# Attention decode over two caches: wo one place further on in the load queue, one exp a tile with a masked copy, both q in SBUF, score sums two chunks behind

## The chip, the cores and the metric

The kernel runs on one core of one Trainium2 chip. The time is the device time of one execution in microseconds (us). Medians of several executions are given, beside executions of the kernel before on the same chip in the same rounds. The engines are PE (TensorE matmul), PEld (its weight loads), DVE (VectorE), ACT (ScalarE), POOL (GpSimd) and SP, whose queue (SPq) issues the loads.

## The reference

Two independent attention layers, A and B, each with its own input, caches and weights. For each of 8 batch rows there is one query position, 32 heads of 128, and a cache of 4096 keys and values per head, all in bf16.

```python
def _A_ref(x, k_cache, v_cache, wq, wo):          # B is the same
    q = (x @ wq).reshape(B, 1, H, Dh).transpose(0, 2, 1, 3)
    scores = einsum("bhqd,bhkd->bhqk", q, k_cache) * (Dh ** -0.5)
    p = softmax(scores, axis=-1)
    o = einsum("bhqk,bhkd->bhqd", p, v_cache)
    return o.transpose(0, 2, 1, 3).reshape(B, 1, H * Dh) @ wo
return concatenate([a, b], axis=-1)
```

Nearly all of the 1.1 GB that the kernel reads are the two caches, and each byte of them is used once.

## The kernel before

The work is cut into 64 tiles, n = 0 to 63 (0 to 31 are cache A). A tile is 8 heads of one batch row: a K tile and a V tile, each of 128 partitions x 64 KB, 8.39 MB. SBUF holds three slots of that size. Two take K tiles in turn (and now and then a weight), the third takes V tiles (the very last V tile goes into a K slot). All loads go through one queue, in the order of a plan that is laid down at the start. A load is issued when the last reader of its slot is done, and a load that has to wait holds up all loads behind it in the plan.

The plan before. The output weight `wo` of a cache takes a K slot, once its last full block of tiles is done. The last K tile and the last V tile are loaded in pieces (`cuts`), and between the pieces of the last V comes `wo8`, the rows of wo for the last 8 heads:

```python
put("wq", 0, 1)
put("k", 0)
put("wq", 1, 2)
for n in range(NQ - 1):
    if n + 2 < NQ:
        put("k", n + 1)
    else:
        put("k", n + 1, cuts=((0, NR // 2), (NR // 2, NR)))
    for c in range(NC):
        if n == done_at(c, NC, HB, B) + 1:        # n = 32 for A, 56 for B
            put("wo", c)
            late[n] = c
    put("v", n, 2)
put("v", NQ - 1, cuts=((0, NR // 2),))
put("wo8", 0, 2)                                  # into the V slot
plan.append(("v", NQ - 1, ((NR // 2, 3 * NR // 4), (3 * NR // 4, 7 * NR // 8), (7 * NR // 8, NR))))
```

The load of a tile. `opT[(kind, n, r)]` is the load that a reader of chunk r (of 8) has to await:

```python
for r0, r1 in cuts or ((0, NR),):
    cols = slice(r0 * CT * Dh, r1 * CT * Dh)
    op = dma(to[:, cols], from_[:, cols], (kind + "l", r0) if cuts else key, [dep])
    for r in range(r0, r1):
        opT[(kind, n, r)] = op
...
elif kind == "wo":
    rows = wo_rows(n)                             # 128 for A, 96 for B
    opT[(kind, n)] = dma(to[0:rows, 0:H * D], caches[n][4][0:rows * H, :].rearrange("(p r) n -> p (r n)", r=H), key, [dep])
```

A K tile in 8 chunks: DVE multiplies by q (`ring<-ring,qbc`) and folds 128 to 64, PE sums 64 to 16 into PSUM (`red`), DVE sums the rest (`s_sb<-red`). Two `red` banks are used in turn, and DVE sums a chunk right after it has multiplied the next one. When the tile is done, DVE finds a shift for the softmax, and ACT writes the weights of the tile in eight passes, one for each head, masked by scale and bias:

```python
for j in range(HQ):                               # HQ = 8
    e.activation(PM[:, :, j], s_sb[:, n % 2, :], ACTF.Exp, bias=bias[:, n % 2, j:j + 1],
                 scale=own_sc[:, j:j + 1], accum_out=rsum[:, blk % 2, b, j:j + 1])
```

PV of tile n (64 matmuls of PM with V) runs on PE at chunk 5 of tile n + 1, and the V slot is then free. PV of the last tile runs in four parts, each of which awaits its piece of V:

```python
for g0, g1 in ((0, 8), (8, 12), (12, 14), (14, 16)):
    make_pv(n, g0 * RG // 16, g1 * RG // 16)      # awaits opT[("v", n, g1 * NR // RG - 1)]
```

## Time and profile before

| | before |
|---|---|
| time, median (lowest to highest) of 3 | 2605.85 us (2604.26 to 2607.56) |
| span of the profiled execution | 2604.0 us |
| read from HBM | 1107.3 MB |
| DVE / PE / ACT busy | 81% / 48% / 26% |

Four lines of the page: busy time of the engines; the share of the load engines in tenths and the GB/s that they moved, both in 40 slices of 65 us; and their packets and bytes in all.

```profile
PE 1256.4 (48%) x8130; PEld 387.1 (15%) x8130; DVE 2103.5 (81%) x1807; ACT 675.6 (26%) x1169; POOL 5.7 (0%) x23
...
DMA  9999999999999999999999999999999999999997
GB/s 420 430 433 433 435 431 432 432 430 434 433 434 432 434 435 433 432 432 432 433 406 434 434 432 433 432 433 432 429 433 435 433 432 434 421 320 432 433 426 324
DMA packets 20840, 1108.61 MB, mean 426 GB/s; under 512 B 2272, under 2 KB 2336, under 8 KB 3376
```

The DMA row is at 9 in all slices but the last, and the rate stays at 429 to 435 GB/s but for the first slice, slice 21 (406, A's wo), slices 35 and 36 (421 and 320, B's wo) and the last two. The Trainium skill, "DMA: Bandwidth & Descriptors", "Where 436 GB/s comes from", puts the ceiling of the 16 ports at 435.2 GB/s; the trace agrees, with 433 for hundreds of us. The same section says that for loads from HBM a lower limit, about 358 GB/s, binds; in this trace it did not. So the kernel is bound by its loads.

Three of the groups (line, engine, operation, out<-in, shapes, count | busy us, mean ns of one | idle us before, and on whom):

```profile
L315 DVE TENSOR_TENSOR ring<-ring,qbc 128x4096 bf16<-128x4096 bf16 x512 | 1169.7, 2284 | 334.5 <-DMA ring<-in_B_k_cache_dram 168.8 <-DMA ring<-in_A_k_cache_dram 165.7
...
L356 ACT ACTIVATE PM<-s_sb,bias,own_sc 128x256 bf16<-128x256 f32 x512 | 609.4, 1608 | 935.2 <-DVE bias L349 935.2
L337 DVE TENSOR_REDUCE s_sb<-red 128x32 f32<-128x512 f32 x512 | 350.2, 684 | 126.1 <-PE red L329 126.1
```

DVE waits 334.5 us for K tiles and 126.1 us for PE. ACT's eight exps of a tile are 1.6 us each, and they overlap.

Stretches of the span (from:to, length, busy us of the five engines with instruction counts, granted PE clock, DMA share, GB/s):

```profile
600.00:1000.00 400.00, 194.15 (x1249) 59.35 (x1250) 337.87 (x290) 108.72 (x191) 0.00 (x0) 0.60 1.00 433
1315.00:1320.00 5.00, 3.58 (x57) 1.59 (x50) 3.94 (x4) 0.60 (x1) 0.00 (x0) 1.00 0.84 357
1320.00:1325.00 5.00, 2.10 (x8) 0.51 (x6) 4.97 (x5) 0.00 (x0) 0.00 (x0) 0.93 0.54 236
...
1360.00:1365.00 5.00, 1.04 (x4) 0.31 (x4) 1.12 (x2) 0.00 (x0) 0.00 (x0) 1.00 0.97 419
2275.00:2280.00 5.00, 2.10 (x8) 0.53 (x5) 4.92 (x5) 0.00 (x0) 0.00 (x0) 0.66 0.36 157
...
2290.00:2295.00 5.00, 2.70 (x6) 0.72 (x7) 5.00 (x5) 4.68 (x10) 0.00 (x0) 0.50 0.98 210
...
2330.00:2335.00 5.00, 1.57 (x16) 0.70 (x20) 0.00 (x0) 0.00 (x0) 0.00 (x0) 0.50 0.97 419
2572.00:2576.00 4.00, 1.86 (x12) 0.68 (x10) 3.23 (x3) 0.41 (x1) 0.00 (x0) 1.00 0.79 286
2576.00:2580.00 4.00, 1.41 (x4) 0.43 (x4) 2.53 (x3) 0.00 (x0) 0.00 (x0) 0.62 1.10 412
```

The load engines idle for a few us at 1315 to 1325 and 2275 to 2280, just before A's and B's wo are issued, and a little at 2572. While B's wo is loaded (2280 to 2310, one line of it is shown) they are as busy as ever, but at 210 GB/s.

The moments at which a K tile has landed can be read from DVE, because DVE waits for almost every one: the first multiply of a tile starts when it lands. These are tiles 56, 57, 58 and 59, with B's wo between 57 and 58 (columns: start, us, what, idle before and on whom):

```profile
2242.31 2.29 DVE L315 TENSOR_TENSOR ring<-ring,qbc 128x4096 bf16<-128x4096 bf16 x1 [4.31 <-DMA ring<-in_B_k_cache_dram]
...
2280.99 2.29 DVE L315 TENSOR_TENSOR ring<-ring,qbc 128x4096 bf16<-128x4096 bf16 x1 [1.03 <-DMA ring<-in_B_k_cache_dram]
...
2352.83 2.29 DVE L315 TENSOR_TENSOR ring<-ring,qbc 128x4096 bf16<-128x4096 bf16 x1 [29.76 <-DMA ring<-in_B_k_cache_dram]
...
2391.54 2.29 DVE L315 TENSOR_TENSOR ring<-ring,qbc 128x4096 bf16<-128x4096 bf16 x1 [3.84 <-DMA ring<-in_B_k_cache_dram]
```

An ordinary interval is 38.7 us, the time of one K and one V. Across B's wo it is 71.8 us.

And the end of the span, in order of time (first the two PV of tiles 62 and 63 and the issue of wo8 between them; then the first and the last exp of tile 63, from ACT's own timeline):

```profile
2566.23 5.54 PE L368 MATMUL pv<-ring,PM 128*32 128x512 bf16 x64 [1.45 <-DMA ring<-in_B_v_cache_dram]
...
2571.81 0.38 SPq L162 DMA_DIRECT2D ring<-in_B_wo_dram  x1
...
2592.60 6.00 PE L368 MATMUL pv<-ring,PM 128*32 128x512 bf16 x64
```

```profile
2582.48 1.52 ACT L356 ACTIVATE PM<-s_sb,bias,own_sc 128x256 bf16<-128x256 f32 x1 [10.07 <-DVE bias L349]
...
2590.32 1.60 ACT L356 ACTIVATE PM<-s_sb,bias,own_sc 128x256 bf16<-128x256 f32 x1
```

The last exp ends near 2592, after the loads have ended (about 2590); only then comes the last PV, 6.0 us for all 64 matmuls.

### The profile page before, as it was taken

The page shows a single profiled execution, that of the slowest core. Times are in us where ns is not written, and L with a number is a line of the kernel's source. Part 1 is how long each engine was busy: PE and PEld are TensorE (multiplying, and loading weights), DVE is VectorE, ACT ScalarE, POOL GpSimd, SP SyncE. Part 2 cuts the span into 40 slices and gives each one's busy share as a digit, 9 for nine tenths or more (in the row PEclk, how much of TensorE's full clock was granted, in tenths as well). Part 3 has the DMA queues.
Part 4 walks back from the last instruction along what each step waited for, and adds up shares of the span by engine and source line. Part 5 has one row for each costly group of instructions (what it writes and reads, how often), then busy time and mean ns, then how long its engine had stood idle before and what let it go on. Part 6 is the DMA issues. An engine that isn't in the chain of part 4 may idle for free.

```text
span 2604.0 us, 19575 instructions
## 1 busy us (share of the span) xinstructions
PE 1256.4 (48%) x8130; PEld 387.1 (15%) x8130; DVE 2103.5 (81%) x1807; ACT 675.6 (26%) x1169; POOL 5.7 (0%) x23
## 2 busy tenths in 40 slices
PE   3554454454454454455454544544545544543454
PEld 1111111111111111111111111111111111111111
DVE  3788888888888888889886888888888888857885
ACT  1223223223223223213312232232232232213133
POOL 0000000000000000000000000000000000000000
PEclk8665665665665665665566556656656656655666
DMA  9999999999999999999999999999999999999997
GB/s 420 430 433 433 435 431 432 432 430 434 433 434 432 434 435 433 432 432 432 433 406 434 434 432 433 432 433 432 429 433 435 433 432 434 421 320 432 433 426 324
DMA packets 20840, 1108.61 MB, mean 426 GB/s; under 512 B 2272, under 2 KB 2336, under 8 KB 3376
## 3 DMA queue, kind: packets, MB, share of 16 engines
q1 hardware_dynamic: 20656, 1107.32, 99.1%
q8 instruction: 63, 1.03, 0.2%
q14 instruction: 25, 0.20, 0.0%
q10 hardware_dynamic: 96, 0.05, 0.0%
HBM read 1107.33 MB, written 0.03 MB: 425 GB/s over the span
## 4 chain that ended last, share of the span: by engine, by line
DMA 53%; DVE 32%; PE 13%; ACT 2%; issue 1%; DVEq 0%
DMA ring<-in_A_k_cache_dram 26%; DMA ring<-in_B_k_cache_dram 24%; DVE ring L315 16%; DVE ring L320 10%; PE pv L368 6%; PE red L329 6%; DVE s_sb L337 5%; ACT PM L356 1%; DMA ring<-in_B_wo_dram 1%; DMA ring<-in_B_v_cache_dram 1%; DMA ring<-in_A_wq_dram 1%; PE q L279 1%; DVE rmax L343 1%; DVE rtmp L345 0%; DVE bias L349 0%
## 5 line engine op out<-in xcount | busy, mean ns | idle before, releaser
L329 PE MATMUL red<-ring,ident 128*128 128x512 bf16 x2048 | 851.3, 562 | 1265.3 <-DVE ring L320 1265.3
L315 DVE TENSOR_TENSOR ring<-ring,qbc 128x4096 bf16<-128x4096 bf16 x512 | 1169.7, 2284 | 334.5 <-DMA ring<-in_B_k_cache_dram 168.8
L356 ACT ACTIVATE PM<-s_sb,bias,own_sc 128x256 bf16<-128x256 f32 x512 | 609.4, 1608 | 935.2 <-DVE bias L349 935.2
L320 DVE TENSOR_TENSOR ring<-ring 128x2048 bf16<-128x2048 bf16 x512 | 621.9, 1215 | 0.0
L329 PEld LDWEIGHTS red<-ring,ident 128*128 128x128 bf16 x2048 | 204.3, 121 | 1807.6 <-DVE ring L320 1541.8
L337 DVE TENSOR_REDUCE s_sb<-red 128x32 f32<-128x512 f32 x512 | 350.2, 684 | 126.1 <-PE red L329 126.1
L368 PE MATMUL pv<-ring,PM 128*32 128x512 bf16 x4096 | 318.0, 479 | 16.6 <-DMA ring<-in_B_v_cache_dram 16.6
L356 ACT ACTIVATION_READ_ACCUMULATOR PM<-s_sb,bias,own_sc 128x1 f32 x512 | 256.0, 500 | 0.0
L376 ACT ACTIVATE accS<-pv 128x512 bf16<-128x512 f32 x64 | 38.2, 597 | 819.7 <-PE pv L368 819.7
L368 PEld LDWEIGHTS pv<-ring,PM 128*32 128x32 bf16 x4096 | 121.5, 118 | 233.7 <-issue 178.8
L305 ACT ACTIVATE qbc<-misc 128x128 bf16<-128x128 f32 x64 | 17.8, 278 | 136.3 <-PE misc L300 136.3
L389 PE MATMUL o<-accS,E 128*32 128x32 bf16 x896 | 31.7, 177 | 0.0
L279 PE MATMUL q<-ring,xT 128*8 128x512 bf16 x128 | 26.1, 423 | 11.2 <-DMA ring<-in_A_wq_dram 11.2
L389 PEld LDWEIGHTS o<-accS,E 128*32 128x32 bf16 x896 | 25.9, 94 | 24.2 <-ACT accS L376 23.3
L343 DVE TENSOR_REDUCE rmax<-s_sb 128x1 f32<-128x256 f32 x64 | 26.9, 420 | 2.2
L300 PE MATMUL misc<-q_sb,selb 8*32 8x128 bf16 x512 | 26.2, 295 | 0.8 <-ACT q_sb L288 0.8
L345 DVE TENSOR_SCALAR rtmp<-half,rmax 128x32 f32<-128x32 f32 x64 | 15.4, 241 | 2.3
L288 ACT ACTIVATE q_sb<-q 8x512 bf16<-8x512 f32 x16 | 9.3, 603 | 30.7 <-PE q L279 30.6
L300 PEld LDWEIGHTS misc<-q_sb,selb 8*32 8x32 bf16 x512 | 9.2, 103 | 53.9 <-issue 53.9
L349 DVE SCALAR_TENSOR_TENSOR bias<-own_sc,ngm,own_b 128x8 f32<-128x8 f32 x64 | 14.5, 226 | 2.3
L407 PE MATMUL o<-rsum,own_m 128*32 128x8 f32 x112 | 7.1, 202 | 18.2 <-ACT PM L356 18.2
L348 DVE TRANSPOSE_TENSOR_REDUCE ngm<-rtmp 128x1 f32<-128x32 f32 x64 | 13.5, 211 | 2.2
(37 smaller groups left out, 55.7 us busy)
## 6 DMA issues: line engine op xcount, KB each, us to landing
ring<-in_B_k_cache_dram SPq DMA_DIRECT2D x2, 4096.0 KB, 35.6
ring<-in_B_v_cache_dram SPq DMA_DIRECT2D x1, 4096.0 KB, 32.0
ring<-in_B_wo_dram SPq DMA_DIRECT2D x1, 2048.0 KB, 10.2
ring<-in_B_v_cache_dram SPq DMA_DIRECT2D x1, 2048.0 KB, 14.7
ring<-in_B_v_cache_dram SPq DMA_DIRECT2D x2, 1024.0 KB, 17.0
ring<-in_A_k_cache_dram SPq DMA_DIRECT2D x32, 41.3
ring<-in_A_v_cache_dram SPq DMA_DIRECT2D x32, 30.3
ring<-in_B_k_cache_dram SPq DMA_DIRECT2D x31, 41.0
```

Source lines behind the costliest of these rows:

```text
L279: i = e.matmul(q_ps[f][rows, :], xT[:, (c * DC + k) * B:(c * DC + k + 1) * B], w[:, col:col + 512], start=(k == 0), stop=(k == DC - 1), ti ...
L300: x = e.matmul(misc[32 * g:32 * (g + 1), 0:Dh], selb[rows, b, i, :], q_sb[rows, j * Dh:(j + 1) * Dh], start=(i == 0), stop=(i == 1), tile_ ...
L305: "act", lambda e: e.activation(qbc[:, n % 2, :], misc[:, 0:Dh], ACTF.Copy),
L315: opMul[s] = add("dve", lambda e: e.tensor_tensor(v, v, qbc[:, n % 2, :].unsqueeze(1).to_broadcast([128, CT, Dh]), ALU.mult), [opT[("k", n ...
L320: return add("dve", lambda e: e.tensor_tensor(v[:, :, 0:64], v[:, :, 0:64], v[:, :, 64:128], ALU.add), [opMul[s]])
L329: i = e.matmul(dst, ident[:], v[:, :, j, :], start=(j == 0), stop=(j == 3))
L337: opRed[s] = add("dve", lambda e: e.tensor_reduce(s_sb[:, n % 2, r * CT:(r + 1) * CT], red_ps[s % 2][:, :].rearrange("p (t w) -> p t w", w ...
L343: opRmax[n] = add("dve", lambda e: e.tensor_reduce(rmax[:], s_sb[:, n % 2, :], AX.X, ALU.max), [opRed[NR * n + NR - 1]])
L356: return e.activation(PM[:, :, j], s_sb[:, n % 2, :], ACTF.Exp, bias=bias[:, n % 2, j:j + 1], scale=own_sc[:, j:j + 1], accum_out=rsum[:, ...
L368: i = e.matmul(pv_ps[32 * q:32 * (q + 1), :], PM[:, t:t + 4, :].rearrange("p t j -> p (t j)"), v[:, t * Dh:(t + 4) * Dh], start=(g == 0), ...
L376: opAcc[n] = [add("act", lambda e: e.activation(accS[:], pv_ps[:], ACTF.Copy), [opPV[n], _at(opExt, n - 1)])]
L389: x = e.matmul(o_ps[MB * hb:MB * (hb + 1), H * b:H * (b + 1)], E[:, i, PH - 1 - u:PH - 1 - u + MB], accS[:, i * 128 + H * u:i * 128 + H * ...
```

## The change

In words: wo one place further on, behind the V tile; one exp a tile into `pe`, and a masked copy of it on DVE; q of both caches computed early and kept in SBUF; score sums two chunks behind, over four PSUM banks; PV in two halves. The intent is to take the wait of wo off the head of the queue, to shorten the softmax and to take DVE's waits for PE away. The diff, cut to what can touch the time:

```diff
@@ the plan @@
+            put("v", n, 2)
             for c in range(NC):
                 if n == done_at(c, NC, HB, B) + 1:
                     put("wo", c)
-                    late[n] = c
-            put("v", n, 2)
+                    late[n + 2] = c
@@ the loads @@
                     for r0, r1 in cuts or ((0, NR),):
                         ...
-                        for r in range(r0, r1):
+                        for r in range(H):
                             opT[(kind, n, r)] = op
@@ sums @@
-        red_ps = [ps(f"red{i}") for i in range(2)]
+        red_ps = [ps(f"red{i}") for i in range(4)]
...                                   # red of chunk s - 2 behind the multiply of chunk s (was s - 1)
@@ softmax @@
-            for j in range(HQ):
-                def emit(e, j=j):
-                    return e.activation(PM[:, :, j], s_sb[:, n % 2, :], ACTF.Exp, bias=bias[:, n % 2, j:j + 1],
-                                        scale=own_sc[:, j:j + 1], accum_out=rsum[:, blk % 2, b, j:j + 1])
+            opExp[n] = add("act", lambda e: e.activation(pe[:], s_sb[:, n % 2, :], ACTF.Exp, bias=ngm[:, n % 2:n % 2 + 1], scale=scale,
+                                                         accum_out=rsum[:, blk % 2, b:b + 1]), ...)
+            opPM[n] = add("dve", lambda e: e.tensor_tensor(PM[:], pe[:].unsqueeze(2).to_broadcast([128, T, HQ]),
+                                                           own_h[:].unsqueeze(1).to_broadcast([128, T, HQ]), ALU.mult), ...)
@@ row sums of the last block: eight matmuls instead of one @@
@@ PV @@
-        pv_at = {((n + 2, 0) if n in late else (n + 1, 5)): n for n in range(NQ - 1)}
+        pv_at = {(n + 1, 5): n for n in range(NQ - 1)}
-                if k == 0:
-                    make_pv(v, 0, RG)
-                    make_acc(v)
+                if k < 2:                         # half at chunk 5, half at chunk 6
+                    make_pv(v, k * RG // 2, (k + 1) * RG // 2)
@@ the product with wo @@
-            if r >= 5 and n - 1 in late:
-                i = r - 5
-                make_proj(late[n - 1], i * H // 3, (i + 1) * H // 3)
+            if r == 0 and n in late:
+                make_proj(late[n])
... # q of both caches: make_q interleaves the four head blocks, both caches at the start
```

## The prediction

> **What bounds the kernel now.** The stream from HBM. The page's DMA row shows 1108.6 MB; windows of 400 us in the middle move 432 to 433 GB/s at a DMA share of 1.00, so the bytes alone take about 2560 of the 2604 us span. DVE is busy 81%, PE 48%, ACT 26%. The timeline shows a tile pair (one K, one V) every 38.7 us. DVE works on a K tile for about 35 us, then waits for the next: 334.5 us in all (groups), some 4.6 us for an ordinary tile. The queue always has work: a K load is issued 41 us and a V load 30 us before it lands, with 22 and 11 us of other loads ahead of it. So a faster DVE, PE or ACT cannot show there.
>
> The other 44 us (narrow windows) are mostly:
> - B's wo load of 96 rows: 6.3 MB at 210 GB/s, DMA share near 1.0, 30 us in place of 14.5: 15.5 us lost. The change keeps it.
> - The queue running dry before each wo (share 0.54 at 1320 to 1325, 0.36 at 2275 to 2280): wo waits for the K tile in work, and V waits behind it. By the landings of K, about 2 us lost in A, 3 in B.
> - The tail: the last V lands near 2590, the span ends 14 us later. The last softmax ran eight exps in a row (9.5 us), so all of the last PV (6.0 us) came after the loads.
>
> **What the change does.**
> 1. wo behind V(n): V's 19 us cover the wait. Both dry spells go: -5 us.
> 2. Eight exps (1.14 us from start to start) become one, about 1.6 us: off the critical path but in the last tile.
> 3. The masked copy is a DVE tensor_tensor of 128x2048 whose first input repeats one element 8 times. The Trainium skill, "Vector Engine (DVE) Microarchitecture Reference", 5.1, measured such a stepless input at 1x. Nothing in this trace shows it; its 2x ops take 2284 ns for 4096 elements, so 2048 at 1x should take about 2.28 us: +146 us of DVE, less 14.5 us for the bias op.
> 4. Sums lagging two chunks over four PSUM banks: most of DVE's 126 us of waits for PE go. With 3, DVE per tile stays near 35 us of 38.7; busy rises to about 2235 us (86%).
> 5. PV in two halves: V is issued about 3.5 us later, against 11 us of cover.
> 6. q of both caches early: matmuls of four column groups interleave, 64 in about 6 us instead of 14.4. Hidden: K lands at 43 us.
> 7. Tail: exp 1.6 + copy 2.3 replace 9.5; the last lsum grows to eight fp32 matmuls (estimate 4 us, partly under the copy). PV ends 5 to 6 us earlier: -5.5 us.
>
> **Predicted: 2596 us**, range 2588 to 2604. Chances: faster by over 2% 1%, within 2% 97%, slower 2%.
>
> **What would show it right or wrong.** DMA share about 1.0 around both wo issues; wo of B still 30 us; middle windows still 433 GB/s; masked copy 2.28 us; DVE wait for K 4 to 5 us a tile; DVE waits for PE under 40 us; last V landing to the end about 8 us instead of 14.
>
> **What would make it wrong.** The later V issue meeting DMA engines that have run dry [...]: 1 us a tile gives 2650. A copy over 3.5 us would make DVE the limit.

## The result

| | before | after |
|---|---|---|
| time, median (lowest to highest) of 4 each | 2605.45 us (2604.26 to 2607.56) | 2612.85 us (2612.49 to 2613.43) |
| ratio | | 1.0028 (95% interval 1.001 to 1.0045) |
| span of the profiled execution | 2604.0 us | 2611.2 us |
| DVE busy | 2103.5 us | 2221.5 us |
| ACT busy | 675.6 us | 105.2 us |

A ratio is the mean time of one kernel's runs over the mean of the other's from the same rounds, so it is not quite the ratio of the medians. The change makes the kernel slower by 7.4 us, 0.28%, which is within 2% but outside the predicted 2588 to 2604.

The page after:

```profile
PE 1221.1 (47%) x8046; PEld 371.0 (14%) x8046; DVE 2221.5 (85%) x1805; ACT 105.2 (4%) x273; POOL 5.7 (0%) x23
...
GB/s 418 434 434 434 433 433 433 432 432 433 433 432 431 433 432 433 429 428 433 432 403 435 434 434 435 431 432 432 432 433 433 432 432 432 432 304 432 426 430 292
```

The rate is the same in the middle. It is lower than before in slice 36 (304 for 320), where B's wo is loaded, and in the last slice (292 for 324).

The groups that answer to those of before:

```profile
L311 DVE TENSOR_TENSOR ring<-ring,qbc 128x4096 bf16<-128x4096 bf16 x512 | 1169.3, 2284 | 351.8 <-DMA ring<-in_B_k_cache_dram 187.2 <-DMA ring<-in_A_k_cache_dram 164.6
...
L333 DVE TENSOR_REDUCE s_sb<-red 128x32 f32<-128x512 f32 x512 | 348.6, 681 | 1.4 <-PE red L325 1.4
...
L353 DVE TENSOR_TENSOR PM<-pe,own_h 128x2048 bf16<-128x2048 bf16 x64 | 146.2, 2284 | 0.7 <-ACT pe L347 0.7
...
L347 ACT ACTIVATE pe<-s_sb,ngm 128x256 bf16<-128x256 f32 x64 | 32.5, 509 | 1032.7 <-DVE ngm L344 1032.7
...
L347 ACT ACTIVATION_READ_ACCUMULATOR pe<-s_sb,ngm 128x1 f32 x64 | 11.9, 187 | 0.0
```

DVE's waits for PE have gone from 126.1 to 1.4 us. The masked copy takes 2284 ns, and the exp 0.51 us with 0.19 us for reading the accumulator. DVE still waits 351.8 us for K. The same stretches after (but for 2290 to 2295, with 2580 to 2584 added):

```profile
600.00:1000.00 400.00, 190.25 (x1221) 56.68 (x1222) 356.59 (x290) 15.04 (x41) 0.00 (x0) 0.60 1.00 434
1315.00:1320.00 5.00, 4.21 (x56) 1.72 (x54) 5.00 (x4) 0.60 (x1) 0.00 (x0) 1.00 1.06 459
1320.00:1325.00 5.00, 1.04 (x4) 0.31 (x4) 2.27 (x3) 0.00 (x0) 0.00 (x0) 0.89 0.97 419
...
1360.00:1365.00 5.00, 2.02 (x23) 0.77 (x20) 3.32 (x3) 0.00 (x0) 0.00 (x0) 0.98 0.30 131
2275.00:2280.00 5.00, 1.25 (x13) 0.41 (x9) 2.55 (x3) 0.00 (x0) 0.00 (x0) 0.96 0.98 419
...
2330.00:2335.00 5.00, 0.00 (x0) 0.00 (x0) 0.00 (x0) 0.00 (x0) 0.00 (x0) 0.50 0.74 210
2572.00:2576.00 4.00, 2.95 (x16) 0.88 (x20) 4.00 (x4) 0.00 (x0) 0.00 (x0) 0.50 0.82 352
2576.00:2580.00 4.00, 4.00 (x56) 1.54 (x52) 4.00 (x4) 0.00 (x0) 0.00 (x0) 0.93 0.19 78
2580.00:2584.00 4.00, 1.52 (x16) 0.56 (x8) 4.00 (x4) 0.60 (x1) 0.00 (x0) 0.92 0.54 121
```

The idle stretches at 1315 to 1325 and 2275 to 2280 are gone, as predicted. But there is a new one at 1360 to 1365 (share 0.30), a smaller one at 2330 to 2335 (0.74), and a large one at 2576 to 2584. The K tiles 56 to 59 land so:

```profile
2242.83 2.29 DVE L311 TENSOR_TENSOR ring<-ring,qbc 128x4096 bf16<-128x4096 bf16 x1 [3.99 <-DMA ring<-in_B_k_cache_dram]
...
2281.54 2.29 DVE L311 TENSOR_TENSOR ring<-ring,qbc 128x4096 bf16<-128x4096 bf16 x1 [3.99 <-DMA ring<-in_B_k_cache_dram]
...
2355.63 2.29 DVE L311 TENSOR_TENSOR ring<-ring,qbc 128x4096 bf16<-128x4096 bf16 x1 [38.02 <-DMA ring<-in_B_k_cache_dram]
...
2395.01 2.29 DVE L311 TENSOR_TENSOR ring<-ring,qbc 128x4096 bf16<-128x4096 bf16 x1 [4.66 <-DMA ring<-in_B_k_cache_dram]
```

The interval across B's wo is 74.1 us and not 71.8. The end of the span:

```profile
2550.08 2.29 DVE L311 TENSOR_TENSOR ring<-ring,qbc 128x4096 bf16<-128x4096 bf16 x1 [4.07 <-DMA ring<-in_B_k_cache_dram]
...
2578.49 1.91 PE L365 MATMUL pv<-ring,PM 128*32 128x512 bf16 x32
...
2580.45 0.38 SPq L160 DMA_DIRECT2D ring<-in_B_wo_dram  x1
...
2589.11 2.29 DVE L353 TENSOR_TENSOR PM<-pe,own_h 128x2048 bf16<-128x2048 bf16 x1 [0.67 <-ACT pe L347]
...
2589.14 3.58 PE L408 MATMUL o<-rsum,own_m 128*128 128x8 f32 x16 [2.39 <-ACT pe L347]
...
2600.73 5.17 PE L365 MATMUL pv<-ring,PM 128*32 128x512 bf16 x64 [8.01 <-DMA ring<-in_B_v_cache_dram]
```

Two things are to be seen here that before did not have. DVE waits 4.07 us for the last K tile (2550.08), though its first half is a load of its own; run 1 below starts on that half 34.6 us after the landing of tile 62, without a wait, and after only after 38.8 us. And the last PV, whose weights are ready at 2591.4 (2589.11 + 2.29), waits until 2600.73 and then runs in one piece; before, it was laid out in four parts for four pieces of V.

Where the 7.2 us between the two profiled spans lie, by the landings of K: the start -0.8, across A's wo (tile 32 to 35) +1.3, across B's wo (tile 56 to 59) +3.0, from the landing of tile 62 (2507.65 before, 2511.29 after) to the end +3.6 (96.35 and 99.9 us); the ordinary intervals nothing.

### The profile page after: what moved, and what is told of

It reads as the page before. It is cut to its first block, busy times and chain, and to the rows that moved or that the text cites. A ratio compares the mean times of both kernels' runs of the same rounds, so it can differ in the third digit from the quotient of the medians.

```text
span 2611.2 us, 18455 instructions
## 1 busy us (share of the span) xinstructions
PE 1221.1 (47%) x8046; PEld 371.0 (14%) x8046; DVE 2221.5 (85%) x1805; ACT 105.2 (4%) x273; POOL 5.7 (0%) x23
## 4 chain that ended last, share of the span: by engine, by line
DMA 52%; DVE 44%; PE 2%; issue 1%; another core or an unknown queue 0%; SPq 0%; ACT 0%; DVEq 0%
DMA ring<-in_B_k_cache_dram 26%; DMA ring<-in_A_k_cache_dram 25%; DVE ring L311 23%; DVE ring L316 12%; DVE s_sb L333 6%; DVE PM L353 3%; PE red L325 2%; DMA ring<-in_B_v_cache_dram 1%; DVE rmax L339 1%; PE pv L365 0%; DVE rtmp L341 0%; DVE ngm L344 0%; SPq L160 0%; DVE on_sb L420 0%
## 5 line engine op out<-in xcount | busy, mean ns | idle before, releaser
L311 DVE TENSOR_TENSOR ring<-ring,qbc 128x4096 bf16<-128x4096 bf16 x512 | 1169.3, 2284 | 351.8 <-DMA ring<-in_B_k_cache_dram 187.2
L325 PE MATMUL red<-ring,ident 128*128 128x512 bf16 x2048 | 834.4, 553 | 1334.7 <-DVE ring L316 1334.0
L353 DVE TENSOR_TENSOR PM<-pe,own_h 128x2048 bf16<-128x2048 bf16 x64 | 146.2, 2284 | 0.7 <-ACT pe L347 0.7
L365 PEld LDWEIGHTS pv<-ring,PM 128*32 128x32 bf16 x4096 | 113.5, 114 | 223.2 <-issue 174.4
L347 ACT ACTIVATE pe<-s_sb,ngm 128x256 bf16<-128x256 f32 x64 | 32.5, 509 | 1032.7 <-DVE ngm L344 1032.7
L431 PE MATMUL proj<-ring,on_sb 128*8 128x256 bf16 (+1 forms) x256 | 12.5, 384 | 18.1 <-DMA ring<-in_B_wo_dram 16.7
L275 PE MATMUL o<-ring,xT 128*8 128x512 bf16 x64 | 7.2, 627 | 11.0 <-DMA ring<-in_A_wq_dram 11.0
L347 ACT ACTIVATION_READ_ACCUMULATOR pe<-s_sb,ngm 128x1 f32 x64 | 11.9, 187 | 0.0
```

Of the source, the lines that this page charges most:

```text
L311: opMul[s] = add("dve", lambda e: e.tensor_tensor(v, v, qbc[:, n % 2, :].unsqueeze(1).to_broadcast([128, CT, Dh]), ALU.mult), [opT[("k", n ...
L325: i = e.matmul(dst, ident[:], v[:, :, j, :], start=(j == 0), stop=(j == 3))
L347: opExp[n] = add("act", lambda e: e.activation(pe[:], s_sb[:, n % 2, :], ACTF.Exp, bias=ngm[:, n % 2:n % 2 + 1], scale=scale, accum_out=rs ...
L353: opPM[n] = add("dve", lambda e: e.tensor_tensor(PM[:], pe[:].unsqueeze(2).to_broadcast([128, T, HQ]), own_h[:].unsqueeze(1).to_broadcast( ...
L365: i = e.matmul(pv_ps[32 * q:32 * (q + 1), :], PM[:, t:t + 4, :].rearrange("p t j -> p (t j)"), v[:, t * Dh:(t + 4) * Dh], start=(g == 0), ...
```

## The experiments

All runs gave correct outputs. They were run in three groups, each with its own runs of the kernel before, and after in a fourth; "before" in the table is the median of the group. Between the groups the median of before differs by up to 0.9 us, and an interval of a ratio is some 3 us wide to each side, so a difference of 1 us between medians says little.

| run | time | before | ratio |
|---|---|---|---|
| 1 after, waits by piece again | 2604.89 | 2605.36 | 0.9999 (0.9987 to 1.0012) |
| 2 before, with the widened waits | 2608.78 | 2605.36 | 1.0012 (1.0 to 1.0025) |
| 3 after, wo ahead of V again | 2611.08 | 2605.36 | 1.0023 (1.001 to 1.0035) |
| 4 run 1, B's wo as 128 rows | 2591.93 | 2605.36 | 0.9948 (0.9935 to 0.9962) |
| 5 run 1, wo ahead of V, product in thirds | 2600.91 | 2606.14 | 0.9980 (0.9968 to 0.9993) |
| 6 run 1, PV whole | 2605.57 | 2606.14 | 1.0000 (0.9986 to 1.0013) |
| 7 run 4, K behind wo in halves | 2588.50 | 2606.14 | 0.9933 (0.992 to 0.9945) |
| 8 run 7, wo8 last | 2583.64 | 2606.14 | 0.9915 (0.9901 to 0.9928) |
| 9 after, waits by piece for K alone | 2609.37 | 2606.21 | 1.0010 (0.9996 to 1.0024) |
| 10 after, waits by piece for V alone | 2608.26 | 2606.21 | 1.0009 (0.9996 to 1.0021) |
| 11 run 5, B's wo as 128 rows | 2593.51 | 2606.21 | 0.9950 (0.9937 to 0.9962) |

And from the profiled executions the time from the landing of one K tile to that of another, with three tile pairs and a wo between them, and the time from the landing of tile 62 to the end. Before and run 2 have the same program up to the last tiles, and so have after and runs 1, 9 and 10; within these the first two columns differ by up to 1.0 us, so one such figure is good to about 1 us.

| | A: K 32 to 35 | B: K 56 to 59 | K 62 to the end |
|---|---|---|---|
| before | 137.4 | 149.2 | 96.4 |
| run 2 (before's order) | 138.2 | 149.0 | 99.7 |
| after | 138.7 | 152.2 | 99.9 |
| run 1 (after's order) | 138.8 | 151.4 | 92.2 |
| run 9 (after's order) | 139.1 | 151.8 | 97.9 |
| run 10 (after's order) | 138.6 | 151.2 | 97.0 |
| run 6 (run 1, PV whole) | 137.3 | 153.6 | 91.8 |
| run 3 (before's order) | 142.3 | 147.2 | 100.3 |
| run 5 (before's order) | 138.8 | 147.3 | 92.2 |
| run 4 (after's order, 128 rows) | 139.6 | 138.0 | 93.1 |
| run 11 (before's order, 128 rows) | 139.6 | 141.1 | 91.8 |
| run 7 (run 4, K in halves) | 136.6 | 136.5 | 91.9 |
| run 8 (run 7, wo8 last) | 136.6 | 136.5 | 87.8 |

**Theory and rivals.** Theory: two things cost time. The widened waits stretch the end, and wo behind V does not spare the queue its dry spell but moves it to the next K load, and makes B's slow wo slower. Rivals: the end is longer because of the new work in it (eight row sum matmuls, 3.58 us, and the copy); and the intervals across wo are longer because DVE has more work a tile.

### Run 1: the waits put back

```diff
-                        for r in range(H):
+                        for r in range(r0, r1):
                             opT[(kind, n, r)] = op
```

> The change with one line put back: each piece of a tile that is loaded in pieces is again awaited for itself, not the last piece for all. Theory D (the widened waits make the tail long): the first half of the last K is used 4 us earlier, wo8 is issued before the queue runs dry (2576 to 2582 in the trace after), and only the last eighth of the last PV comes after the last landing, so end minus the last V landing falls from 10.5 us to about 6 us. Time 9 us under the kernel after, about 2604 us, about 1.5 us under before. Rival S (the tail is long because of the new last row sums, 3.6 us on PE, and the copy on DVE): the time moves by less than 2 us from the kernel after.

Measured: 2604.89 us, 8.0 us less than after, 0.9999 of before. The end of the span in this run:

```profile
2575.61 0.38 SPq L160 DMA_DIRECT2D ring<-in_B_wo_dram  x1
...
2583.56 3.58 PE L408 MATMUL o<-rsum,own_m 128*128 128x8 f32 x16 [2.39 <-ACT pe L347]
...
2587.08 5.31 PE L365 MATMUL pv<-ring,PM 128*32 128x512 bf16 x48
...
2592.90 0.62 PE L365 MATMUL pv<-ring,PM 128*32 128x512 bf16 x8 [0.51 <-DMA ring<-in_B_v_cache_dram]
...
2595.33 0.61 PE L365 MATMUL pv<-ring,PM 128*32 128x512 bf16 x8 [1.81 <-DMA ring<-in_B_v_cache_dram]
```

The last PV now runs in parts, and the part behind the last landing is 8 matmuls (0.61 us). From there to the end it is 6.8 us (2602.1 - 2595.33); after had 10.5. wo8 is issued at 2575.61 and not at 2580.45 (65.7 and not 69.2 us after the landing of tile 62). The row sums are still there (2583.56, 3.58 us) and cost nothing, because the last pieces of V land later. The rival for the end is refuted; the theory's 9 us were 8.

### Runs 9 and 10: which of the two waits

```diff
# run 9                                                          # run 10: "v" for "k"
-                        for r in range(H):
+                        for r in range(r0, r1) if kind == "k" else range(H):
```

> The change with the waits put back for the last K tile alone; V still waits for its last piece. Theory D splits the 8 us of the first run: the DVE chain of the last tile starts 4 us earlier, so wo8 is issued 4 to 5 us earlier and everything behind it comes earlier; the last PV still comes whole (5 us) after the last landing. About 4 us under the kernel after, 2609 us. If the waits on V were the whole cost: 2613.

> The change with the waits put back for the last V tile alone. Theory D: the last PV is again taken in pieces as they land, about 4.5 us less after the last landing, while the queue still runs dry before wo8 (2576 to 2582): about 4 us under the kernel after, 2608 to 2609 us. Together with the run before it 8 us.

Measured: 2609.37 and 2608.26 us, 3.5 and 4.6 us less than after by the medians, together 8.1, against 8.0 of run 1; by the ratios it is 4.7 and 5.0 against 7.6. So within the noise the two add up to run 1, and the split between them is rough. Both waits cost, each by its own way, and the traces show both. The wait on K puts off the last tile on DVE, with it the PV of tile 62, with that wo8, and the queue runs dry: without it (run 9) wo8 is issued 65.3 us after the landing of tile 62, and the share at 2576 to 2580 is 0.77; with it (run 10) 70.0 us and 0.02. The wait on V puts the whole last PV behind the last landing: run 9 still ends with all 64 matmuls (5.16 us at 2596.36), run 10 with 8 (1.05 us at 2598.97).

### Run 2: the widened waits in the kernel before

> The kernel before with the widened waits alone. Theory D: it loses little, since its last softmax hides the last V anyway: the last K waits about 2 us more, so +2 us, 2607 to 2608. If the widened waits cost the same in every kernel, +9 us, about 2614.

Measured: 2608.78 us, +3.4 us. The cost is less than half of what the same line costs after the change. In before the last softmax ends after the loads anyway, so there is nothing left for the wait on V to put off (in run 2 the loads end near 2592.4 and the last PV starts at 2595.63). What is left is the wait on K, with about the cost that run 9 found for it; it was not tried alone in before. The two parts of the change therefore do not add: the shorter softmax makes the last landing the critical one, and the widened wait sits right on it.

### Run 3: wo ahead of V again, first try

```diff
-            put("v", n, 2)
             for c in range(NC):
                 if n == done_at(c, NC, HB, B) + 1:
                     put("wo", c)
-                    late[n + 2] = c
+                    late[n] = c
+            put("v", n, 2)
...            # PV of that tile at (n + 2, 0) as before, the product with wo in one lump at chunk 7
```

> The change with wo in its old place, ahead of V (and the late PV of that tile, as before). Theory W (the dry spell only moved, from the wo issue to the next K issue, and got longer): K landing intervals across wo go back from 60.3 to about 59.0 us (A) and from 74.1 to about 72 us (B), so 3 to 4 us under the kernel after, about 2609 us. Rival P (the intervals are longer because DVE has 2.3 us more work a tile): they stay at 60.3 and 74.1 and the time stays at 2613.

Measured: 2611.08 us, 1.8 us less than after; the prediction of it was 3 to 4. The run was not clean. Across B's wo it won 5 us (147.2 us from K 56 to 59, after 152.2), but across A's it lost 3.6 (142.3 for 138.7), because the product in one lump on PE delayed the last sums of a K tile and so the next K load (issued at 1367.3, before at 1361.9). Run 5, which takes the product in three parts, is back at 138.8 across A's.

### Run 5: the same, cleanly

Run 1 with wo ahead of V, PV of that tile late, and the product with wo in three parts at chunks 5 to 7, all as in before. These come as a set and were not tried apart.

> The first run (waits put back) with wo ahead of V as before, and now also the output product in three parts at chunks 5 to 7 as before, which the run with wo first lacked (its product in one lump held up the next K load, 1367 in place of 1362). Theory W (the new place of wo is worth nothing, and costs where wo is slow): the two K intervals up to the K behind B's wo sum to 108 to 110.5 us against 112.6 in the first run, A's stay at 99 to 100; time 2 to 4 us under the first run, about 2602 us. Rival: the order makes no difference, the time stays at 2605.

Measured: 2600.91 us and a ratio of 0.9980 against 0.9999 of run 1, so 5 us less by the ratios (4.0 by the medians; run 6, of the same group and in after's order, took 4.7 more). Across A's wo nothing changes (138.8 and 138.8), across B's it is 147.3 against 151.4. The new place of wo brings nothing in A and costs 4 us in B. The rival that DVE's extra work makes the intervals longer is refuted for B: run 5 has all of that work, and takes 147.3 us where before takes 149.2. In A it is not refuted (138.8 us, against 137.4 in before and 138.2 in run 2), and the trace speaks for it. In tile 33 DVE now does the masked copy (2.3 us) and the output's scaling (1.5 us); the load of K 34, which needs the slot of K 33, is issued 37.2 us after the landing of K 33, in run 5 as in after, where before has 33.9. So run 5, in before's order, has a dry spell at 1360 to 1365 too (share 0.57; before 0.97). What is left of the change without the widened waits and without the new order is worth 5.2 us (2600.91 against 2606.14).

### Run 4: B's wo as 128 rows

```diff
# on top of run 1
-                    rows = wo_rows(n)
+                    rows = 128                   # 32 rows more than are used
```

> The change with the waits put back as in the first run, and B's wo loaded as all 128 rows though only 96 are used: a third more bytes. If the 96-row load is slow by its shape (210 GB/s), it now takes about 19.4 us instead of 30 to 34, the K interval across B's wo falls from 74.1 to about 60.3 us, and the time is 11 to 14 us under the first run, about 2591 us. If the load is slow for another reason (place in the queue, the stalled PE), the time is 5 us over the first run.

Measured: 2591.93 us, 13 us less than run 1, with 2.1 MB more loaded. From K 56 to 59 it is 138.0 us instead of 151.4. The load of 96 rows is slow by its shape: it moved 210 GB/s at a share near 1.0. The Trainium skill, "SBUF — State Buffer", "Door 1: The DMA port swizzle", says that the rate depends on how many of the 16 ports a transfer's partitions reach, and gives 8 ports about 218 GB/s; under "The DMA setup-cost knee" it advises to use 128 partitions. The page has no case of 96; the 210 GB/s measured here are near its figure for 64 partitions, though by its port table 96 partitions reach all 16 ports. That the ports are the cause is not shown here, only that the shape is.

### Run 11: both orders with 128 rows

> The run with wo first and its product in thirds, and B's wo loaded as 128 rows. Theory N (the place of wo costs 4 us only because B's load of 96 rows is slow among other loads): the two orders are then alike, so this run equals the run with all rows and wo behind V (2592 us) within 1.5 us, and both wo are crossed in 99 us for two K intervals. Rival (wo behind V costs 4 us whatever its shape): 2588 us.

Measured: 2593.51 us, ratio 0.9950, against 0.9948 of run 4: the two orders are alike in time, as far as intervals of 3 us to each side can tell. So wo behind V costs, as far as was tried, only where the load of wo is the slow one. (In the profiled execution of this run B took 3 us longer than in run 4 and the end 1.3 us less, so the expected 99 us for two intervals was missed, at 99.9 and 101.9; the times do not show it.) The traces show where the 4 us lie. In before wo starts on a queue that has run dry, and the stretch at 210 GB/s lasts from 2280 to 2310 and moves 6.3 MB, just wo. In after, wo follows V without a gap, and the slow stretch lasts from 2295 to 2335, at 215 GB/s: 8.6 MB, so 2.3 MB of the loads next to wo went at the slow rate too. At 433 GB/s these would take 5.3 us and not 10.7, by which we estimate a loss of some 5 us. Why they are slowed with it stays open.

### Run 7: the K tile behind wo in halves

```diff
# on top of run 4; early = the K tiles that go into the slot of the K tile in work (34 and 58)
+                if kind == "k" and n in early:
+                    dep = opEacc.get(NR * (n - 1) + cuts[0][1] - 1)   # half the old tile is used up
```

> The run with all 128 rows, and the K tile behind each wo loaded in halves, the first as soon as the first half of the K tile in its slot is used up. Theory M (the dry spell moved from the wo issue to this K issue): the share of 0.30 at 1360 to 1365 and 0.46 at 2315 to 2320 goes to about 1, the K interval across each wo falls from 60.5 to 61 to about 58.5 us; 4 to 5 us under the run with all rows, about 2587 us. Rival (the queue's dry spell is only uneven engines, the slowest never stops): no change, 2592.

Measured: 2588.50 us; by the ratios (0.9933 and 0.9948) 3.9 us less than run 4. The two stretches in run 4, and then in run 7:

```profile
1360.00:1365.00 5.00, 2.60 (x23) 0.93 (x21) 3.38 (x3) 0.14 (x1) 0.00 (x0) 0.80 0.30 131
2315.00:2320.00 5.00, 2.02 (x11) 0.65 (x9) 3.06 (x3) 0.29 (x1) 0.00 (x0) 0.87 0.46 197
```

```profile
1360.00:1365.00 5.00, 2.65 (x22) 0.87 (x20) 3.00 (x3) 0.04 (x1) 0.00 (x0) 0.82 0.99 426
2315.00:2320.00 5.00, 3.10 (x28) 1.21 (x32) 1.15 (x2) 0.00 (x0) 0.00 (x0) 0.55 0.96 413
```

With half the slot given free early, the load engines no longer stop. So the dry spell at this place is this wait, of the next K load for the K tile in work: while wo holds one K slot, the other cannot be loaded until DVE is done with it, wherever wo stands in the plan. (Run 5 had the spell in before's order; before, where DVE is done 3 us sooner, had none.) Over the three intervals A fell from 139.6 to 136.6 us and B from 138.0 to 136.5; the single interval of the expectation can't be compared, because the first half of that K tile is now awaited by itself.

### Run 6: PV whole

```diff
-                if k < 2:
-                    make_pv(v, k * RG // 2, (k + 1) * RG // 2)
+                if k == 0:
+                    make_pv(v, 0, RG)
```

> The first run (waits put back) with PV whole at chunk 5 again in place of two halves. Theory H (the halves put off the end of PV, so the loads that wait for its V slot): V is issued about 29 us after K lands and not 32, nothing changes in the middle, wo8 is issued 2 us earlier and the dry spell before it at the end shrinks; 1 to 2 us under the first run, about 2603 us. If the halves cost nothing anywhere: 2605.

Measured: 2605.57 us, ratio 1.0000 against 0.9999: no difference. The mechanism is there but small: wo8 was issued 63.6 us after the landing of tile 62 and not 65.7, and the end was 0.4 us shorter (91.8 for 92.2), which is within the noise. Across A's wo it took 1.5 us less and across B's 2.2 us more; this was not followed up. In the time, the halves of PV are not a cause of the loss.

### Run 8: wo8 behind the last V

> The run before this one, and wo8 loaded behind the last V instead of before its second half, so that no load waits for the last but one PV. The queue should no longer run dry at the end, and the last PV comes while wo8 is loaded: 5 to 6 us under the run before this one, about 2581 us. If the end is bound by the chain of the last tile on DVE and not by loads: less than 2 us.

```diff
# on top of run 7
-        put("v", NQ - 1, cuts=((0, NR // 2),))
+        put("v", NQ - 1, cuts=((0, NR // 2), (NR // 2, 3 * NR // 4), (3 * NR // 4, 7 * NR // 8), (7 * NR // 8, NR)))
         put("wo8", 0, 2)
-        plan.append(("v", NQ - 1, ((NR // 2, 3 * NR // 4), (3 * NR // 4, 7 * NR // 8), (7 * NR // 8, NR))))
```

Measured: 2583.64 us, 4.9 us less than run 7. This is the best version found: 22.5 us (0.85%) less than before and, by its ratio and that of after, about 1.1% less than after. The last V no longer waits for the PV of tile 62, and the last PV (at 2570.0, all 64 matmuls) runs while wo8 is still loading.

## Why the prediction was wrong

The prediction was 2596 us, and the time is 2612.85. The missing 17 us are three terms.

1. **A line of the diff was not read: +8 us that the sum did not have.** Step 7 says that the last PV ends "5 to 6 us earlier: -5.5 us". It took for granted that the last PV still follows the landing of V in pieces. `range(H)` took that away. Run 1 puts the line back and gains 8.0 us; runs 9 and 10 split it into 3.5 (K) and 4.6 (V). Without it the predicted mark "last V landing to the end about 8 us" is met (6.8 us); with it, it was 10.5.
2. **Step 1, "Both dry spells go: -5 us", had the wrong sign: +5 us.** The two spells did go where they were predicted to go, but the first came back at the next K load (share 0.30 at 1360 to 1365), and in B the slow load held up more of its neighbours. By run 5 against run 1 the new order costs 4 to 5 us, which by the traces lies at B's wo. The prediction had weighed the wait of wo for its slot, and not the wait of the K load behind it for the only slot left. Its own figures held the warning: a K tile takes DVE about 35 us and two loads take 38.7 us, which left under 4 us. In after that K load was issued 37.2 us after the landing of the K tile before it, which left 1.5; and a load does not land in one moment: in before, the 16 signals of an ordinary K load come over 7 us (from the records of the packed trace). Step 3 had a part in it: the masked copy lies in these 37.2 us.
3. **Step 7's size.** With the waits put back, the time from the landing of tile 62 to the end is 92.2 us and not 96.4, 4.2 us less for the predicted 5.5. Part of the difference may be a dry spell before wo8: V is issued later, as step 5 had said, and with it wo8 (65.7 us after the landing of tile 62, before 64.2); run 6 gets no more than 0.4 us of it back.

The terms, with the measured ones beside: order -5 predicted, +5 measured; the rest of the change -5.5 predicted, -5.2 measured (run 5 against before); the widened waits 0 predicted, +8 measured. The measured terms give +7.8 us, against +7.4 of the medians; as each term is the step from one run of the chain to the next, they must add up, and the sum is no further proof. That the rest is so near its prediction is in part luck: by the traces the end gave 4.2 us of it, B 1.9, which no step had foreseen, and A took 1.4 back.

What was right:

- The loads bind, and the middle moves 433 to 434 GB/s before and after. DVE's 118 us of additional work, ACT's 570 us less and the 125 us of waits that DVE lost moved none of the ordinary intervals of 38.7 us (across A's wo DVE's work is felt, see run 5).
- The masked copy takes 2284 ns; 2.28 us was predicted from the 2x ops of the trace and from the Trainium skill, "Vector Engine (DVE) Microarchitecture Reference", 5.1, where an op with two inputs of 2 bytes an element, one of which repeats an element 16 times, ran at 1x. The trace agrees, here with 8 repeats: 2048 elements take as long as 4096 in the multiply by q.
- DVE's waits for PE fell to 1.4 us (under 40 predicted), its wait for K stayed at 4 to 5 us a tile, and its busy time is 2221.5 us (2235 predicted). The row sums took 3.58 us (4 estimated).
- One size was missed without harm: the exp took 0.51 + 0.19 us and not 1.6.
- B's wo kept its slow rate.

## What to carry to other kernels

In a kernel that is bound by its loads, look at each load for what its slot waits on, and follow the wait to the next load that the freed or taken slot sets up: moving one load in the queue moves the dry spell unless the slot comes free earlier. Read the lines of a change that set what is awaited as closely as those that compute; one range that was too wide cost more here (8 us) than the change without it and without the new order gained (5 us). And when a load is far under the rate of its neighbours at the same busy share, try its full 128 partitions, even if some of the bytes are not wanted.

## What the Trainium skill lacked or had wrong

- "SBUF — State Buffer", "Door 1: The DMA port swizzle": no case of 96 partitions. By its port table 8 ports would get 8 of these rows each, as with 128 rows, and 8 ports get 4, so that one would estimate about 19.4 us for B's wo (8.39 MB at 433 GB/s, the time of a full tile); it took about 30 us at 210 GB/s. With 128 rows the three intervals across it fell from 151.4 to 138.0 us.
- "DMA: Bandwidth & Descriptors", "Why a DMA increments its semaphore by 16 and not by 1": it says that a tile of 96 partitions goes over all 16 engines. The DMA share near 1.0 agrees with that, but the page has no rate for 96 partitions; here the engines were all busy at half the rate of their neighbours (210 against 433 GB/s).
- "ScalarE: Activation LUTs", "What ACT_TABLE_LOAD costs": it gives an ACTIVATE whose bias is a pointer operand as 280 ns + 0.833 ns an element, and 93 ns more for a second pointer. By it, as an estimate, the exp of after (256 elements a partition, bias by pointer) should take 493 ns, and the trace has 509; one exp of before (scale and bias by pointer) should take 586 ns, and the trace has 1608 ns, with 1.12 us from start to start ((2590.32 - 2582.48) / 7). Two things that the page has no figure for are in the slow form: it writes every eighth element, and its reading of the accumulator takes 0.5 us and not 0.19. Which of them costs the time was not tried.
